# Planned attention steps with loads, first splits and conversions in the list, new due dates, and seven of ten banks of a pair split on GpSimd

## The chip, the cores and the metric

The kernel runs on one core of a Trainium2 chip. Its time is the device time of one execution in microseconds (us); less is better. Engines are called PE (matrix), DVE (vector), ACT (scalar), POOL (GpSimd) and SP (which issues the DMAs).

## What is computed

```python
scores = scale * np.matmul(q, k.transpose(0, 1, 3, 2))        # q, k, v: 4 x 8 heads x 576 x 64
thresh = np.max(scores, axis=-1, keepdims=True) - tau
scores = np.where(scores >= thresh, scores, -1000000000.0)
attn = softmax(scores)                                        # exp, sum, divide
x = (attn @ v), heads put side by side                        # 2304 tokens x 512
x = (silu(x @ w_gate) * (x @ w_val)) @ w_out                  # inner width 1536
out = (((x @ w1) * (x @ w2)) @ w3) @ w_out2                   # inner width 1024
```

The weights arrive as 64-bit floats, so each block of them is rebuilt as 32-bit values on the chip ("conversion"). Every matmul operand is split into a rounded part (hi) and the rest (lo), and products are summed from two or three matmuls.

## The kernel before

Attention takes two heads at a time, a *pair*: 16 pairs (4 batches of 4), 9 tiles of 128 query rows in each (four of head 0, one of both heads' last 64 rows, four of head 1), 144 tiles in all. A tile's chain is: `mm_scores` on PE into one of two double banks (L539), `el_max` on DVE (L571), the threshold (L580), `el_mask` on DVE (L587), which frees the bank, and `el_exp` on ACT (L596). A pair's probabilities are then transposed on PE (L425) into ten single banks, in the order four of head 0, `lq`, `kl`, four of head 1, and each bank is split into hi and lo in AT or ATL by one of three *paths*, named by one letter of `ROWS` (`plan_evac`):

- X: ACT copies hi (L891), DVE subtracts (L895);
- Y: ACT copies the bank to a tmp (L878), POOL rounds it (L184) and subtracts (L189);
- Z: ACT copies hi, PE subtracts it in the bank (`less`, L432), ACT copies lo (L902).

`plan_pv` then multiplies with v (L946, L958), ACT copies the result (L971), and SP stores it. For the next pair, `plan_turn` transposes q and k on PE, ACT makes hi (L813), DVE makes lo (L819), and `stack` issues four DMAs for k into R and eight for q into L (L448, L449), from which the next pair's scores read. `plan_left` does the last 64 rows of q and k, from `qkls`, which is split once in four pairs. `plan_split_v` splits v on POOL.

The order of all this, from the first pair's scores to the second tile of the last pair, comes from a list. `make_plan` gives each step an engine, a time for which it holds the engine (`busy`), a time after which its result may be used (`until`), the steps it waits for and a due date, counted in tiles (`z` is the pair's first tile). `Plan.order` goes through time and lets each engine take, among its next `AHEAD` steps by due date, the one that can start first, and of several the one that is due first:

```python
first = min(r[0] for r in ready)
t, due, k, step = min(
    (r for r in ready if r[0] <= first), key=lambda r: r[1:3]
)
```

The steps are then emitted in that order. On the chip each engine works through its own instructions in order and waits where an input isn't there. Ahead of the list stands a prologue (L756 to L772): the first loads, `first` (both heads of pair 0's k and q are split on DVE, transposed, copied to L and R), `split_left` and `it_left`. The last pair and everything behind it are emitted item by item. `plan_conv` is a weight block's conversion: an int part on DVE (L225, L228, L231), two activations on ACT, a subtract on POOL, a value on DVE (L257), a copy and a subtract (L299); three of the conversions (`EARLY`) stand in the list. Their loads are issued by `conv_fetch` within `begin` and `end`.

Of the kernel before, what the change touches and what calls it, by code (L numbers as in the profile page):

```python
# [33 lines left out]
ROWS, LAST = ("YZYYYXYYZX",), "XZ"  # L34


class Plan:
# [3 lines left out]
    HOP, AHEAD = 0.06, 60  # L41
# [16 lines left out]
    def order(self):  # L58
# [24 lines left out]
        while any(queues.values()):  # L83
            best = None
            for engine, q in queues.items():
                ready = []
                for due, k, step in q[:self.AHEAD]:
                    t = earliest(step, free[engine])
                    if t is not None:
                        ready.append((t, due, k, step))  # L90
                if not ready:
                    continue
                first = min(r[0] for r in ready)
                t, due, k, step = min(
                    (r for r in ready if r[0] <= first), key=lambda r: r[1:3]
                )
                if best is None or t < best[0]:
                    best = (t, engine, due, k, step)
# [15 lines left out]
def kernel(  # L114
# [177 lines left out]
    def conv_unit(src, key, **kw):  # L292
        def done(val):
# [5 lines left out]
            eng.tensor_tensor(out=un[:, 1, :], in0=val, in1=f32(un[:, 0, :]), op=ALU.subtract)  # L299
            wu[key] = un  # L300
        conv_push(src, done, **kw)
# [31 lines left out]
    def attention(actx, early, tail):  # L333
# [23 lines left out]
        def load_left(b):  # L357
            qk = ld.tile([P, H, D], F32, tag="qkl", name="qkl", bufs=1)
            vl = ld.tile([P, HP, D], F32, tag="vl", name="vl", bufs=1)
            nc.sync.dma_start(out=qk[0:64], in_=q[b, :, 512:S, :].rearrange("h p d -> p h d"))  # L360
            nc.sync.dma_start(out=qk[64:128], in_=k[b, :, 512:S, :].rearrange("h p d -> p h d"))
            vs = v[b, :, 512:S, :].rearrange("(g e) p d -> e p g d", e=2)
            for e in range(2):
                nc.sync.dma_start(out=vl[64 * e:64 * e + 64], in_=vs[e])
            lraw[b] = (qk, vl)
# [16 lines left out]

        def split_left(b):
            qk, vl = lraw.pop(b)
            qks = sp.tile([P, H, 3, D], F32R, tag="qkls", name="qkls", bufs=1)
            eng = nc.gpsimd if b else nc.vector
            for e in (0, 2):
                eng.tensor_scalar(
                    out=qks[:, :, e, :], in0=qk, scalar1=1.0, scalar2=1.0,
                    op0=ALU.mult, op1=ALU.mult,  # L390
                )
            eng.tensor_tensor(
                out=qks[:, :, 1, :], in0=qk, in1=f32(qks[:, :, 0, :]), op=ALU.subtract
            )
            for h in range(2):
                r = slice(64 * h, 64 * h + 64)
                split_pool(VLZ[b % 2][r, :, h, 0, :], VLZ[b % 2][r, :, h, 1, :], vl[r])
            lsplit[b] = qks
# [81 lines left out]


        def first(i, scale):
            L, R = qk_tiles(0)
            raw = raws.pop((0, i))
            for h in range(2):
                un = take()
                s5 = un.rearrange("p a b -> p (a b)")[:, 0:12 * D].rearrange(
                    "p (t s d) -> p t s d", t=4, s=3)
                src, hi = raw[:, h, :, :], s5[:, :, 0, :]
                for s in (0, 2):  # L490
                    nc.vector.tensor_scalar(
                        out=s5[:, :, s, :], in0=src, scalar1=scale, scalar2=None, op0=ALU.mult
                    )
                nc.vector.scalar_tensor_tensor(
                    out=s5[:, :, 1, :], in0=src, scalar=scale, in1=f32(hi),
                    op0=ALU.mult, op1=ALU.subtract,
                )
                s0 = (h + i + 1) % 2
                for n, a in enumerate((s0,) if i else (s0, 1 - s0)):
                    turn_r(  # L500
                        [s5[:, t, a:a + 2, :].rearrange("p s d -> p (s d)") for t in range(4)],
                        R[:, 640 * h:640 * h + 512] if i else L[:, 2 * n + h, :],
                    )
                give(un)

        def it_left(p):
            b, hp = divmod(p, HP)
            L, R = qk_tiles(p)
            qks = lsplit[b]
            bank = t_bank()  # L510
            br = bank.bitcast(F32R)
            for e in range(2):
                for h in range(2):
                    c = (2 * e + h) * P
                    s0 = (e + h + 1) % 2
                    src = qks[:, 2 * hp + h, s0:s0 + 2, :].rearrange("p a d -> p (a d)")
                    nc.tensor.transpose(br[:, c:c + P], src, ident_r)
            lz = LZ.rearrange("p e (h c) -> p e h c", c=192)[:, :, :, 0:64]
            bv = bank.rearrange("p (e h c) -> p e h c", e=2, h=2)
            scaled(lz, bv[:, :, :, 0:64], q_scale)  # L520
            scaled(R[:, 512:640].rearrange("p (h c) -> p h c", h=2), bv[:, 1, :, 64:P])
            scaled(R[:, 2 * S:2 * S + 64], bv[:, 1, 1, 64:P])
# [203 lines left out]
        def prep_items(p):  # L726
            b, hp = divmod(p, HP)
            return [lambda f=f: f(p) for f in (it_k, it_q, it_left)]

        def split_items(p):  # L730
            return [lambda: split_left(p // HP)] if p % HP == 0 else []

# [17 lines left out]
        def run_item(f):  # L750
# [4 lines left out]

        load(0, (1, 0))  # L756
        load_left(0)
        nc.scalar.dma_start(out=tau_sb, in_=tau.to_broadcast([P, 1]))

        nc.vector.tensor_scalar(  # L760
            out=q_scale, in0=tau_sb, scalar1=0.0, scalar2=0.125 / FAR, op0=ALU.is_ge, op1=ALU.mult
        )
        nc.vector.tensor_scalar(
            out=tau_sb, in0=tau_sb, scalar1=0.0, scalar2=None, op0=ALU.max
        )
# [102 lines left out]
        def plan_evac(path, b, a, due, hi, lo):  # L868
            if path == "Y":
                k = {}  # L870

                def raw():
# [18 lines left out]
                "ACT", 0.47, 0.6, [a], lambda: nc.scalar.copy(out=hi, in_=b["t"]), due + 0.1  # L891
            )
            if path == "X":
# [3 lines left out]
                    ), due + 0.3, closes=b,  # L897
                )
                return [c, d]
            d = plan.add("PE", 0.23, 0.45, [c], lambda: less(b["t"], hi), due + 0.2)  # L900
            e = plan.add(
                "ACT", 0.47, 0.6, [d], lambda: nc.scalar.copy(out=lo, in_=b["t"]), due + 0.3,  # L902
# [119 lines left out]
        def plan_split_left(b, due, war):  # L1022
            k = {}

            def qk_round(e):
                if not k:
                    k["qk"], k["vl"] = lraw.pop(b)
                    lsplit[b] = sp.tile([P, H, 3, D], F32R, tag="qkls", name="qkls", bufs=1)
                pool_round(lsplit[b][:, :, e, :], k["qk"])

            a = plan.add("POOL", 0.59, 0.63, war, lambda: qk_round(0), due)
            c = plan.add("POOL", 0.59, 0.63, [a], lambda: qk_round(2), due)
            d = plan.add("POOL", 1.25, 1.3, [c], lambda: pool_rest(
                lsplit[b][:, :, 1, :], k["qk"], lsplit[b][:, :, 0, :]), due)
            last = [d]
            for h in range(2):
                r = slice(64 * h, 64 * h + 64)
                hi, lo = (VLZ[b % 2][r, :, h, e, :] for e in range(2))
                last.append(plan.add(
                    "POOL", 0.38, 0.43, [last[-1]],  # L1040
                    lambda hi=hi, r=r: pool_round(hi, k["vl"][r]), due + 6 + h))
                last.append(plan.add(
                    "POOL", 0.72, 0.76, [last[-1]],
                    lambda hi=hi, lo=lo, r=r: pool_rest(lo, k["vl"][r], hi), due + 6 + h))
            return d, last[-1]

        def plan_split_v(p, due, war):
# [10 lines left out]
            if p + 2 < NP:  # L1058
                plan.add("SP", 0.1, 3.0, [c], lambda: load(p + 2, (2,)), due + 0.1)
            return c  # L1060

        def plan_conv(due):
# [7 lines left out]
            def end():  # L1070
# [552 lines left out]
```

## Time and profile before

| what | us |
|---|---|
| median of 3 runs | 1174.66 (1173.36 to 1178.68) |
| the profiled execution | 1175.01 |
| its span, first to last instruction | 1173.2 |
| PE busy / DVE busy / ACT busy / POOL busy | 1106.8 / 736.4 / 577.1 / 485.5 |

The span is 1.8 us shorter than the profiled execution's own time. "Busy" is the time in which an engine had an instruction under way; for PE the ends of matmuls are modelled, so a busy PE is not one at its peak. Attention is roughly the first 345 us; the rest are the two feed-forward stages.

### The profile page before, as it was taken

The page shows a single profiled execution, that of the slowest core. Times are in us where ns is not written, and L with a number is a line of the kernel's source. Part 1 is how long each engine was busy: PE and PEld are TensorE (multiplying, and loading weights), DVE is VectorE, ACT ScalarE, POOL GpSimd, SP SyncE. Part 2 cuts the span into 40 slices and gives each one's busy share as a digit, 9 for nine tenths or more (in the row PEclk, how much of TensorE's full clock was granted, in tenths as well). Part 3 has the DMA queues.
Part 4 walks back from the last instruction along what each step waited for, and adds up shares of the span by engine and source line. Part 5 has one row for each costly group of instructions (what it writes and reads, how often), then busy time and mean ns, then how long its engine had stood idle before and what let it go on. Part 6 is the DMA issues. An engine that isn't in the chain of part 4 may idle for free.

```text
span 1173.2 us, 16903 instructions
## 1 busy us (share of the span) xinstructions
PE 1106.8 (94%) x6008; PEld 957.4 (82%) x6008; DVE 736.4 (63%) x1300; ACT 577.1 (49%) x1151; POOL 485.5 (41%) x463
## 2 busy tenths in 40 slices
PE   5888899899988999999999999999899999999998
PEld 4778789898976877888888888888778888888886
DVE  6798999898885896756463655477991122522223
ACT  4687788888876356443341423245662231321111
POOL 2577587777643655443232333233332221321110
PEclk9898999999998999999999999999999999999999
DMA  4775766667655842222020211123330010100023
GB/s 99 176 179 129 174 153 165 161 144 171 144 176 137 237 117 90 72 72 72 19 72 19 68 58 36 42 84 113 111 112 7 1 37 1 37 1 1 1 61 101
DMA packets 105331, 107.09 MB, mean 91 GB/s; under 512 B 48288, under 2 KB 79648, under 8 KB 105248
## 3 DMA queue, kind: packets, MB, share of 16 engines
q1 hardware_dynamic: 105104, 106.01, 34.2%
q8 instruction: 48, 0.79, 0.3%
q14 instruction: 35, 0.29, 0.1%
q10 hardware_dynamic: 144, 0.00, 0.0%
HBM read 68.16 MB, written 14.23 MB: 70 GB/s over the span
## 4 chain that ended last, share of the span: by engine, by line
PE 55%; DVE 5%; DMA 1%; issue 1%; ACT 0%; POOL 0%; DVEq 0%; ACTq 0%
PE t_bank L1327 36%; PE s_bank L1327 19%; DMA raw<-in_moe_w_dram 1%; DVE tmp L257 1%; DVE slot L1310 1%; DVE raw L228 1%; DVE tmp L231 1%; DVE tmp L225 0%; DVE slot L1403 0%; DVE slot L299 0%; DVE slot L1512 0%; DVE slot L1374 0%; PE t_bank L1400 0%; DVE slot L1549 0%; POOL slot L299 0%
## 5 line engine op out<-in xcount | busy, mean ns | idle before, releaser
L1327 PE MATMUL t_bank<-slot,slot 128*128 128x512 f32 (+1 forms) x2592 | 561.3, 372 | 5.8 <-ACT slot L1309 2.0
L1327 PEld LDWEIGHTS t_bank<-slot,slot 128*128 128x128 f32 x2592 | 458.3, 189 | 93.0 <-ACT slot L1309 2.4
L1327 PE MATMUL s_bank<-h,slot 128*128 128x512 f32 (+1 forms) x720 | 163.3, 374 | 4.8 <-ACT h L192 2.9
L245 POOL TENSOR_TENSOR raw<-raw 128x512 int32<-128x512 int32 x76 | 83.6, 1101 | 167.5 <-ACT raw L240 158.2
L1327 PEld LDWEIGHTS s_bank<-h,slot 128*128 128x128 f32 x720 | 127.8, 191 | 29.2 <-ACT h L192 3.6
L1559 DVE TENSOR_TENSOR tmp<-tmp,t_bank 128x512 f32<-128x512 f32 (+1 forms) x40 | 25.3, 633 | 178.2 <-PE t_bank L1327 178.2
L193 POOL TENSOR_TENSOR h<-tmp,h 128x512 fp32r<-128x512 f32 (+1 forms) x60 | 74.4, 1241 | 141.2 <-ACT h L192 140.9
L1563 POOL TENSOR_TENSOR h<-tmp,h 128x512 fp32r<-128x512 f32 (+1 forms) x38 | 45.8, 1206 | 200.4 <-ACT h L1561 200.4
L571 DVE TENSOR_SCALAR_CACHE_REDUCE E<-s_bank 128x576 f32<-128x576 f32 x144 | 107.6, 753 | 32.3 <-PE s_bank L539 31.0
L596 ACT ACTIVATE P<-P,stat 128x576 f32<-128x576 f32 x144 | 113.8, 794 | 20.7 <-DVE P L587 20.0
L539 PE MATMUL s_bank<-R,L 128*128 128x288 f32 x512 | 101.1, 323 | 20.9 <-DVE P L587 11.4
L587 DVE SCALAR_TENSOR_TENSOR P<-E,stat,s_bank 128x576 f32<-128x576 f32 x144 | 114.5, 809 | 1.6
L189 POOL TENSOR_TENSOR AT<-tmp,AT 128x512 fp32r<-128x512 f32 x88 | 113.3, 1303 | 1.8
L1327 PE MATMUL s_bank<-slot,h 128*128 128x512 f32 x432 | 106.6, 391 | 0.9 <-DVE slot L1549 0.8
L1412 DVE TENSOR_TENSOR tmp<-tmp,t_bank 128x512 f32<-128x512 f32 (+1 forms) x60 | 37.9, 631 | 109.2 <-PE t_bank L1327 100.0
L539 PEld LDWEIGHTS s_bank<-R,L 128*128 128x128 f32 x512 | 78.6, 201 | 30.2 <-DVE P L587 9.5
L425 PE MATMUL t_bank<-ident,P 128*128 128x128 f32 x640 | 93.7, 281 | 4.6 <-ACT P L596 2.0
L1327 PEld LDWEIGHTS s_bank<-slot,h 128*128 128x128 f32 x432 | 80.0, 188 | 18.3 <-DVE slot L1549 2.1
L1374 DVE TENSOR_TENSOR slot<-s_bank,slot 128x1024 f32<-128x1024 f32 (+1 forms) x72 | 82.3, 1146 | 18.2 <-PE s_bank L1327 16.1
L184 POOL TENSOR_SCALAR AT<-tmp 128x512 fp32r<-128x512 f32 x88 | 55.2, 639 | 91.5 <-ACT tmp L878 84.3
L257 DVE SCALAR_TENSOR_TENSOR tmp<-tmp,raw 128x512 f32<-128x512 f32 x76 | 69.3, 912 | 34.1 <-POOL raw L245 34.1
L239 ACT ACTIVATE raw<-raw,ebias 128x512 int32<-128x512 int32 x76 | 58.1, 764 | 63.0 <-DVE tmp L231 43.4
(131 smaller groups left out, 1398.8 us busy)
## 6 DMA issues: line engine op xcount, KB each, us to landing
raw<-in_moe_w_dram SPq DMA_DIRECT2D x32, 512.0 KB, 3.6
raw<-in_moe_w_out_dram SPq DMA_DIRECT2D x20, 512.0 KB, 3.5
x_dram<-xs SPq DMA_DIRECT2D x64, 144.0 KB, 2.7
L<-qlo SPq DMA_DIRECT2D x60, 128.0 KB, 2.4
L<-qhi SPq DMA_DIRECT2D x60, 128.0 KB, 2.4
raw<-in_moe_w_gate_dram SPq DMA_DIRECT2D x12, 512.0 KB, 4.1
raw<-in_moe_w_val_dram SPq DMA_DIRECT2D x12, 512.0 KB, 3.5
ld<-in_k_dram SPq DMA_DIRECT2D x16, 256.0 KB, 3.9
```

The lines of the kernel that those rows point to most:

```text
L189: nc.gpsimd.tensor_tensor(out=lo, in0=src, in1=f32(hi), op=ALU.subtract)
L193: nc.gpsimd.tensor_tensor(out=lo, in0=src, in1=f32(hi), op=ALU.subtract)
L239: nc.scalar.activation(out=a, in_=x, func=ACTF.Relu, scale=8.0, bias=ebias[:, 0:1])
L245: nc.gpsimd.tensor_tensor(out=a, in0=a, in1=x, op=ALU.subtract)
L257: nc.vector.scalar_tensor_tensor(out=f32(m), in0=f32(m), scalar=2.0 ** 20, in1=f32(a), op0=ALU.add, op1=ALU.mult)
L425: nc.tensor.matmul(bank[:, t * P:(t + 1) * P], lhsT=part, rhs=ident, is_transpose=True, start=(t == 0), stop=(t == len(parts) - 1),)
L539: nc.tensor.matmul(o, lhsT=lhs, rhs=R[:, c:c + HALF], start=(h == hs2[0] and e == 0), stop=(h == hs2[-1] and e == 1),)
L571: nc.vector.tensor_scalar(out=halves(t), in0=sb[:, :, 0:HALF], scalar1=-FAR, scalar2=None, op0=ALU.mult, op1=ALU.min, accum_out=st[:, 0, c],)
L587: nc.vector.scalar_tensor_tensor(out=halves(p_tile(p, i)), in0=halves(t), scalar=st[:, 1, c], in1=sb[:, :, 0:HALF], op0=ALU.is_gt, op1=ALU ...
L596: nc.scalar.activation(out=u, in_=u, func=ACTF.Exp, scale=-FAR, bias=st[:, 0, c], accum_out=sums[p // HP][:, c],)
L1327: nc.tensor.matmul(o, lhsT=lhs(a), rhs=rhs(c), start=(first and i == 0), stop=(last and i == 2))
L1374: nc.vector.tensor_tensor(out=a, in0=s, in1=a, op=ALU.add)
```

## The change

`ROWS` goes from YZYYYXYYZX to YZYYYZYYYX: of a pair's ten banks, `kl` goes from X to Z, the third bank of head 1 from Z to Y; seven instead of six take path Y, one instead of two path X, two path Z as before. Nearly all due dates are new numbers (the table `W`), and a step is chosen among 400 instead of 60. The prologue is gone: the first loads (k of pair 0, its left rows, q, then v and pair 1's k, q and v), the split of pair 0's k and q head by head, and the left rows' split are steps of the list; two heads of the left rows are split on DVE, the other six and v's left rows on POOL. The first four tiles wait for head 0's operands alone. The next pair's turn of k and q is due about 1.6 and 2.5 tiles earlier. A conversion's load is an SP step of its own, due four tiles ahead, and the last subtract of a conversion is a step of its own on POOL or DVE. The lists' waits for v's loads, and the holding times of the conversion's DVE steps (2.2 for 1.7, 1.0 for 0.6), are new. `load_left` can load q and k's part or v's part alone.

```diff
--- before.py
+++ after.py
-ROWS, LAST = ("YZYYYXYYZX",), "XZ"
+ROWS, LAST = ("YZYYYZYYYX",), "XZ"
+W = {
+    "s": 4.05, "two": 0.98, "exp": 1.03, "k": -0.14, "q": 0.47, "left": 5.44, "sqk": 8.68,
+    "svl": 12.52, "sv": 5.9, "T0": 5, "t0": 0.47, "lq": 7.39, "co": 6.31, "kl": 8.43, "T1": 9.6,
+    "t1": 1.02, "pv": 12.69, "ph": 1.95, "pn": 0.8, "norm": 15.36, "conv": 5.29, "raw": -0.18,
+    "pool": -0.49, "x": -0.09, "z": -1.39,
+}
-    HOP, AHEAD = 0.06, 60
+    HOP, AHEAD = 0.06, 400
...
-                    (r for r in ready if r[0] <= first), key=lambda r: r[1:3]
+                    (r for r in ready if r[0] <= first + 1e-9), key=lambda r: r[1:3]
...
-        load(0, (1, 0))
-        load_left(0)
...
-        first(1, 1.0)
-        first(0, q_scale)
-        split_left(0)
-        it_left(0)
-        load(0, (2,))
-        load(1, (1, 0))
-        load(1, (2,))
...
+        def plan_split_qk(b, due, war, heads, engine, cost):
...
+            a = plan.add(engine, cost, cost + 0.05, war, lambda: both(0), due)
+            c = plan.add(engine, cost, cost + 0.05, [a], lambda: both(2), due)
+            return plan.add(engine, 2 * cost, 2 * cost + 0.1, [c], rest, due)
...
+        def plan_first(i, h, due, deps):
...
+            a = plan.add("DVE", cost, cost + 0.08, deps, lambda: rounds(0), due)
+            c = plan.add("DVE", cost, cost + 0.08, [a], lambda: rounds(2), due)
+            d = plan.add("DVE", 0.34, 0.42, [a], rest, due)
...
+                x = plan_bank(b, due + 0.01 * n, 0.5, [c, d], fill)
...
+                ends.append(plan.add("ACT", 0.47, 0.6, [x], out, due + 0.02, closes=b))
+            return ends, x
+
+        def plan_start():
+            sp_at = lambda cost, land, emit: plan.add("SP", cost, land, [], emit, -20)
+            k0 = sp_at(1.5, 5.1, lambda: load(0, (1,)))
+            l0 = sp_at(0.15, 4.8, lambda: load_left(0, (0,)))
+            q0 = sp_at(0.1, 5.6, lambda: load(0, (0,)))
+            v0 = sp_at(0.15, 6.0, lambda: load_left(0, (1,)))
+            w0 = sp_at(0.1, 6.9, lambda: load(0, (2,)))
+            k1 = sp_at(0.1, 7.8, lambda: load(1, (1,)))
+            q1 = sp_at(0.1, 8.7, lambda: load(1, (0,)))
+            w1 = sp_at(0.1, 9.6, lambda: load(1, (2,)))
...
+            kh0, x = plan_first(1, 0, -8, [k0])
+            left = plan_split_qk(0, -7.5, [l0], slice(0, 2), "DVE", 0.13)
+            qh0, _ = plan_first(0, 0, -7, [q0, qs])
+            left0 = plan_left(0, -6.5, [left])
+            kh1, _ = plan_first(1, 1, -3, [k0])
+            qh1, _ = plan_first(0, 1, -2, [q0, qs, x])
+            rest = plan_split_qk(0, -1, [l0, left], slice(2, H), "POOL", 0.46)
+            vl = plan_split_vl(0, 2, [v0])
+            return kh0 + qh0 + [left0], kh1 + qh1, rest, vl
...
-        def plan_conv(due):
+        def plan_conv(due, engine, deps):
...
-            a = plan.add("DVE", 1.7, 1.8, [], begin, due, opens=r)
+            ld = plan.add("SP", 0.1, 4.5, deps, conv_fetch, due - 4)
+            a = plan.add("DVE", 2.2, 2.3, [ld], begin, due, opens=r)
...
-            e = plan.add("DVE", 0.6, 0.68, [d], end, due + 1)
-            f = plan.add("ACT", 0.47, 0.6, [e], lambda: k["rest"][0](k["val"]), due + 1.2)
-            plan.add("POOL", 1.25, 1.3, [f], None, due + 1.4, closes=r)
+            e = plan.add("DVE", 1.0, 1.1, [d], value, due + 1)
+            f = plan.add("ACT", 0.47, 0.6, [e], copy, due + 1.2)
+            plan.add(engine, 1.25, 1.3, [f], lambda: k["lo"](), due + 1.4, closes=r)
...
-                    score[n] = plan.add("PE", big, big + 0.17, deps, go, n - 3)
+                    score[n] = plan.add("PE", big, big + 0.17, deps, go, n - W["s"])
...
-                rk = plan_turn(q, 1, z + (1.5 if p else 3), soon + ready[p][:1])
-                rq = plan_turn(q, 0, z + (3 if p else 4), soon + ready[p][1:2])
+                rk = plan_turn(q, 1, z + W["k"], soon)
+                rq = plan_turn(q, 0, z + W["q"], soon)
...
-                    lefts[b] = plan_split_left(b, z + 7, [left_done[q], ld])
-                vdone = plan_split_v(p, z + 6, [pv.get(("pv", p - 2)), score[z]])
+                    lefts[b] = plan_split_qk(b, z + W["sqk"], [left_done[q], ld], slice(0, H), "POOL", 0.6)
+                    vls[b] = plan_split_vl(b, z + W["svl"], [ld])
+                vdone = plan_split_v(
+                    p, z + W["sv"], [pv.get(("pv", p - 2)), score[z], landed.get((p, 2))])
...
-                    plan_conv(z + 6)
+                    plan_conv(
+                        z + W["conv"], "DVE" if EARLY.index(p) % 2 else "POOL", [score[z]])
```

## Rows read from the trace of the kernel before

**Rows 1.** The page, part 1: busy us, share of the span, instructions.

```profile
PE 1106.8 (94%) x6008; PEld 957.4 (82%) x6008; DVE 736.4 (63%) x1300; ACT 577.1 (49%) x1151; POOL 485.5 (41%) x463
```

**Rows 2.** Windows: start and end, length, busy by engine, granted clock, DMA share, GB/s.

```profile
0.00:15.52 15.52, 6.35 (x33) 5.18 (x34) 9.03 (x25) 5.32 (x10) 5.53 (x12) 1.00 0.83 167
15.52:36.77 21.25, 13.89 (x77) 12.18 (x77) 14.77 (x36) 11.12 (x28) 7.70 (x9) 0.97 0.37 83
36.77:321.72 284.95, 258.07 (x1898) 244.63 (x1897) 256.59 (x595) 234.30 (x567) 199.22 (x218) 0.96 0.68 158
321.72:345.60 23.88, 21.59 (x146) 19.42 (x145) 21.01 (x47) 18.92 (x45) 12.19 (x11) 1.00 0.59 188
345.60:1173.20 827.60, 806.90 (x3861) 675.98 (x3859) 435.00 (x599) 307.45 (x504) 260.82 (x215) 0.99 0.21 64
```

**Rows 3.** Windows of three single pairs: the fourth, the fifth and the seventh.

```profile
82.41:99.49 17.08, 16.83 (x132) 16.20 (x131) 16.40 (x40) 15.48 (x39) 16.37 (x19) 1.00 0.68 150
99.49:124.76 25.27, 21.86 (x148) 20.62 (x146) 22.07 (x47) 18.16 (x46) 14.63 (x17) 0.86 0.56 127
...
146.83:164.34 17.51, 17.12 (x132) 16.16 (x131) 16.20 (x40) 15.22 (x38) 14.01 (x17) 1.00 0.76 175
```

**Rows 4.** Waits of DVE, 36.77 to 321.72: total us, times, longest.

```profile
DVE E L571 <- PE s_bank L539: 23.9, 31, 3.7
DVE tmp L225 <- DMA raw<-in_moe_w_gate_dram: 2.1, 1, 2.1
```

**Rows 5.** Waits of PE, 36.77 to 321.72: total us, times, longest.

```profile
PE s_bank L539 <- DVE P L587: 18.0, 15, 4.2
PE s_bank L539 <- DMA L<-qlo: 3.0, 3, 1.7
```

**Rows 6.** Timeline where pair 10 begins: start, us, instruction, idle before it.

```profile
225.59 0.66 PE L539 MATMUL s_bank<-R,L 128*128 128x288 f32 x3 [1.67 <-DMA L<-qlo]
...
226.29 0.76 DVE L571 TENSOR_SCALAR_CACHE_REDUCE E<-s_bank 128x576 f32<-128x576 f32 x1 [3.71 <-PE s_bank L539]
```

**Rows 7.** Timeline of pair 0 and the begin of pair 1.

```profile
1.25 0.46 SPq L378 DMA_DIRECT2D ld<-in_q_dram  x1
...
5.23 0.29 DVE L491 TENSOR_SCALAR slot<-ld 128x256 fp32r<-128x256 f32 x1 [1.15 <-DMA ld<-in_k_dram]
...
10.80 0.61 PE L539 MATMUL s_bank<-R,L 128*128 128x288 f32 x1 [0.17 <-ACT L L479]
...
15.52 0.76 DVE L571 TENSOR_SCALAR_CACHE_REDUCE E<-s_bank 128x576 f32<-128x576 f32 x1 [3.50 <-PE s_bank L539]
...
26.75 0.54 SPq L448 DMA_DIRECT2D R<-khi  x1
...
34.44 0.60 SPq L449 DMA_DIRECT2D L<-qhi  x1
...
35.68 1.06 PE L539 MATMUL s_bank<-R,L 128*128 128x288 f32 x3 [2.10 <-DMA L<-qlo]
...
36.77 0.76 DVE L571 TENSOR_SCALAR_CACHE_REDUCE E<-s_bank 128x576 f32<-128x576 f32 x1 [3.32 <-PE s_bank L539]
```

**Rows 8.** Timeline around the first conversion in the list.

```profile
57.71 0.81 DVE L225 TENSOR_SCALAR tmp<-raw 128x512 int32<-128x512 int32 x1 [2.12 <-DMA raw<-in_moe_w_gate_dram]
...
62.37 0.91 PE L539 MATMUL s_bank<-R,L 128*128 128x288 f32 x4 [4.15 <-DVE P L587]
```

**Rows 9.** Single lines, 15 to 322: count, shortest/median/longest ns, first and last start.

```profile
L587 DVE SCALAR_TENSOR_TENSOR P<-E,stat,s_bank x135: 799/809/818, 17.4 to 321.0; 128x576 f32<-128x576 f32 x135
L895 DVE TENSOR_TENSOR AT<-t_bank,AT x14: 678/684/692, 48.0 to 311.3; 128x512 fp32r<-128x512 f32 x14
L184 POOL TENSOR_SCALAR AT<-tmp x85: 611/623/1058, 27.9 to 318.4; 128x512 fp32r<-128x512 f32 x85
L189 POOL TENSOR_TENSOR AT<-tmp,AT x85: 1265/1290/1730, 28.6 to 319.1; 128x512 fp32r<-128x512 f32 x85
L231 DVE SCALAR_TENSOR_TENSOR tmp<-raw,tmp x3: 675/1746/1751, 59.8 to 185.7; 128x512 f32<-128x512 uint16 x3
```

More of the change, by code (lines that the diff above doesn't have):

```diff
@@ L298, in done @@
             eng = nc.gpsimd if conv_i[0] % 2 else nc.vector
-            eng.tensor_tensor(out=un[:, 1, :], in0=val, in1=f32(un[:, 0, :]), op=ALU.subtract)
             wu[key] = un
+            rest = lambda: eng.tensor_tensor(
+                out=un[:, 1, :], in0=val, in1=f32(un[:, 0, :]), op=ALU.subtract
+            )
+            return rest if later else rest()
         conv_push(src, done, **kw)
@@ L355, in attention, with load_left @@
         stats, sums, pbuf = {}, {}, {}
[L357 to L365, printed above, removed]
+        def load_left(b, which=(0, 1)):
+            if 0 in which:
+                t = ld.tile([P, H, D], F32, tag="qkl", name="qkl", bufs=1)
+                nc.sync.dma_start(out=t[0:64], in_=q[b, :, 512:S, :].rearrange("h p d -> p h d"))
+                nc.sync.dma_start(out=t[64:128], in_=k[b, :, 512:S, :].rearrange("h p d -> p h d"))
+                lraw[b, 0] = t
+            if 1 in which:
+                t = ld.tile([P, HP, D], F32, tag="vl", name="vl", bufs=1)
+                vs = v[b, :, 512:S, :].rearrange("(g e) p d -> e p g d", e=2)
+                for e in range(2):
+                    nc.sync.dma_start(out=t[64 * e:64 * e + 64], in_=vs[e])
+                lraw[b, 1] = t
         def load(p, which):
@@ L381, in load @@
                 raws[p, i] = t
[L383 to L398, printed above, removed]
         def split_v(p):
@@ L479, in turn_r @@
             nc.scalar.copy(out=dst, in_=bank)
[L482 to L522, printed above, removed]
         def mm_scores(p, i):
@@ L890, in plan_evac @@
             c = plan.add(
-                "ACT", 0.47, 0.6, [a], lambda: nc.scalar.copy(out=hi, in_=b["t"]), due + 0.1
+                "ACT", 0.47, 0.6, [a], lambda: nc.scalar.copy(out=hi, in_=b["t"]), due + W["raw"]
             )
@@ L896, in plan_evac @@
                         out=lo, in0=b["t"], in1=f32(hi), op=ALU.subtract
[L897 removed]
+                    ), due + W["x"], closes=b,
                 )
                 return [c, d]
[L900 removed]
+            d = plan.add("PE", 0.23, 0.45, [c], lambda: less(b["t"], hi), due + W["z"])
             e = plan.add(
[L902 removed]
+                "ACT", 0.47, 0.6, [d], lambda: nc.scalar.copy(out=lo, in_=b["t"]), due + W["x"],
                 closes=b,
@@ L1020, in plan_norm, with both, rest, plan_split_vl @@
             plan.add("SP", 0.2, 3.0, [d], store, due + 0.2)
[L1022 to L1027, printed above, removed]
-                    lsplit[b] = sp.tile([P, H, 3, D], F32R, tag="qkls", name="qkls", bufs=1)
[L1029 to L1035, printed above, removed]
+        def plan_split_qk(b, due, war, heads, engine, cost):
+            def both(e):
+                if b not in lsplit:
+                    lsplit[b] = sp.tile([P, H, 3, D], F32R, tag="qkls", name="qkls", bufs=1)
+                out, in_ = lsplit[b][:, heads, e, :], lraw[b, 0][:, heads, :]
+                if engine == "POOL":
+                    pool_round(out, in_)
+                else:
+                    nc.vector.tensor_scalar(
+                        out=out, in0=in_, scalar1=1.0, scalar2=None, op0=ALU.mult
+                    )
+            def rest():
+                eng = nc.gpsimd if engine == "POOL" else nc.vector
+                eng.tensor_tensor(
+                    out=lsplit[b][:, heads, 1, :], in0=lraw[b, 0][:, heads, :],
+                    in1=f32(lsplit[b][:, heads, 0, :]), op=ALU.subtract,
+                )
+            a = plan.add(engine, cost, cost + 0.05, war, lambda: both(0), due)
+            c = plan.add(engine, cost, cost + 0.05, [a], lambda: both(2), due)
+            return plan.add(engine, 2 * cost, 2 * cost + 0.1, [c], rest, due)
+        def plan_split_vl(b, due, war):
+            last = war
             for h in range(2):
@@ L1038, in plan_split_left @@
                 hi, lo = (VLZ[b % 2][r, :, h, e, :] for e in range(2))
[L1039 to L1045, printed above, removed]
+                last = [plan.add(
+                    "POOL", 0.38, 0.43, last,
+                    lambda hi=hi, r=r: pool_round(hi, lraw[b, 1][r]), due + h)]
@@ new lines, in plan_split_vl, with rounds, rest, fill @@
+                last = [plan.add(
+                    "POOL", 0.72, 0.76, last,
+                    lambda hi=hi, lo=lo, r=r: pool_rest(lo, lraw[b, 1][r], hi), due + h)]
+            return last[0]
+        def plan_first(i, h, due, deps):
+            k = {}
+            scale = 1.0 if i else q_scale
+            cost = 0.2 if i else 0.26
+            def rounds(s):
+                if not k:
+                    k["un"] = take()
+                    k["s5"] = k["un"].rearrange("p a b -> p (a b)")[:, 0:12 * D].rearrange(
+                        "p (t s d) -> p t s d", t=4, s=3)
+                nc.vector.tensor_scalar(
+                    out=k["s5"][:, :, s, :], in0=raws[0, i][:, h, :, :], scalar1=scale,
+                    scalar2=None, op0=ALU.mult,
+                )
+            def rest():
+                nc.vector.scalar_tensor_tensor(
+                    out=k["s5"][:, :, 1, :], in0=raws[0, i][:, h, :, :], scalar=scale,
+                    in1=f32(k["s5"][:, :, 0, :]), op0=ALU.mult, op1=ALU.subtract,
+                )
+            a = plan.add("DVE", cost, cost + 0.08, deps, lambda: rounds(0), due)
+            c = plan.add("DVE", cost, cost + 0.08, [a], lambda: rounds(2), due)
+            d = plan.add("DVE", 0.34, 0.42, [a], rest, due)
+            s0 = (h + i + 1) % 2
+            ends = []
+            halves_of = (s0,) if i else (s0, 1 - s0)
+            for n, at in enumerate(halves_of):
+                b = plan.res("bank")
+                def fill(bank, n=n, at=at):
+                    for t in range(4):
+                        nc.tensor.transpose(
+                            bank.bitcast(F32R)[:, t * P:(t + 1) * P],
+                            k["s5"][:, t, at:at + 2, :].rearrange("p s d -> p (s d)"), ident_r,
+                        )
+                    if n == len(halves_of) - 1:
+                        give(k["un"])
+                x = plan_bank(b, due + 0.01 * n, 0.5, [c, d], fill)
+                def out(n=n, b=b):
+                    L, R = qk_tiles(0)
+                    dst = R[:, 640 * h:640 * h + 512] if i else L[:, 2 * n + h, :]
+                    nc.scalar.copy(out=dst, in_=b["t"])
+                ends.append(plan.add("ACT", 0.47, 0.6, [x], out, due + 0.02, closes=b))
+            return ends, x
```

84 lines of the change are left out of this document (36 added, 48 removed).

## Prediction

> **What bounds the kernel now.** The page's busy shares come first [rows 1], but they mix two programs: behind 345.6 us PE is busy 806.9 of 827.6 us [rows 2], and nothing of that part is edited. What the change can move lies ahead of it. So the second view is the windows, cut where a pair's first row maximum starts on DVE. Pair 0 takes 36.8 us with everything ahead of it, pairs 1 to 14 take 284.95 us (20.35 each), the last one up to the feed-forward's first stretch 23.9 us [rows 2]. In the fourteen pairs DVE is busy 256.6 of 285 us (90%), PE 258.1 (91%, at a granted clock of 0.96), ACT 234.3 (82%), POOL 199.2 (70%) [rows 2]. No engine is full. The reader is to see two things there: DVE and PE are nearly level, and POOL has 85.7 us left, 6.1 a pair.
>
> The third view is single pairs. The fourth takes 17.08 us and the seventh 17.51, the fifth 25.27, all with the same banks and paths [rows 3]. In the quick ones PE is busy all but 0.25 and 0.4 us, DVE all but 0.7 and 1.3 us [rows 3]. So about 17 us is what the engines' work of a pair takes when the orders fit, and the 3 us between that and 20.35 are waits.
>
> The fourth view says which. DVE waits 23.9 us in 31 places for scores, and 2.1 us for one weight block [rows 4]. PE in turn waits 18.0 us in 15 places for the mask that frees a bank, and 3.0 us for the stacked q [rows 5]: scores late, then masks late, in turns. When PE idles, its clock falls: in the fifth pair it was 0.86 on average, in the quick ones 1.00 [rows 3]. A mean of 0.96 over 285 us, between the levels 1.2 and 2.4 GHz, is 23 us at the lower one (0.04 x 285 / 0.5), in which about 11 us of PE's work is lost. Fewer idles give some of it back.
>
> **The change part by part, worked on the profiled execution, 1175.0 us** (1173.2 of span and 1.8 around it; the median of the runs is 0.35 lower, which is nothing here).
>
> *Paths.* One X less a pair takes one 0.684 us subtract from DVE [rows 9]. The two Z stay two, so PE's and ACT's work is the same: X and Y have one ACT copy each, Z two, twelve before and after. One Y more puts 0.623 + 1.290 = 1.91 us on POOL [rows 9]. On DVE, fourteen pairs make -9.6 us, and with DVE at 90% in a ring with PE I take all of it. POOL goes from 14.2 (199.2 / 14) to 16.1 us a pair; its cover is the 6.1 us of idle, of which 2.5 are left if a pair takes 18.6. The cost is 0 there. If the last split of head 1 ended last ahead of the product with v, it would be 1.91 each pair, 26.7 us in all.
>
> *The banks' split moving to POOL, against a rule.* First the row: with POOL busy 70% of the time, 135 masks took 799 to 818 ns [rows 9], so not one was held up by POOL; the conversion's L231 took 675 at best and 1746 in the middle, and POOL's own two operations reach 1058 and 1730 [rows 9]. So the engines do get in each other's way, but in the conversions' steps. The Trainium skill, page "Perfetto Trace Analysis", section "Optimizing Scalar/DVE Operations", warns that DVE and GpSimd share a port into SBUF, so that moving work from the one to the other may not help. This case's trace agrees for L231 alone, and speaks against it for the masks (799 to 818 ns). The sum goes by the row, 0; by the rule's word 26.7 us would go back on DVE, a rival below.
>
> *Earlier turn of k and q.* Twelve DMAs per pair stay twelve, 7.7 us of SP from the first issue to the last [rows 7], landing after that. Before, they end so late that pair 1's scores wait 2.1 us and DVE 3.3 [rows 7]; in pair 10 PE waits 1.67 and DVE 3.71 [rows 6]. Due two tiles earlier, 4 us at 2.0 to 2.3 us a tile, they should land before the pair begins. What is queued behind them on SP are stores of the results and loads two pairs ahead, which have a pair's time. I take off pair 1's 3.3 (in the start's sum) and 5 us in the fourteen pairs: pair 10's 3.7 and something for the other two waits of PE on q. Bounds: 3 (PE's own waits [rows 5]) and 8.
>
> *Conversions.* Load as a step of its own: the 2.1 us wait of DVE goes [rows 4, 8]; behind it stood a mask, and PE waited 4.15 us for that [rows 8]. The conversion's work stays: three blocks, the same two on POOL and one on DVE. The longer holding times only let the list leave room. I take -2.1, bounds 0 and -4.
>
> *Other due dates, 400 steps in view.* This has no row of its own. Of DVE's 28.4 us of idle (284.95 - 256.59), 2.1 and 5 are gone above; about 21 are left, mostly 0.2 to 2 us each behind scores. Below stands no gain at all; above, all pairs at the mean of the quick ones, 17.3. Scores due four tiles ahead, not three, stand earlier in PE's order, which is what DVE waits for in 31 places; but the wider view also lets work be pulled up whose input on the chip is late. I take -3, near the lower end.
>
> *Start.* Before, the first score starts at 10.8 us and the first maximum at 15.5 [rows 7], because both heads of k and q and the whole of qkls are split first. After, only head 0's k and q, and two heads of the left rows. The counter-cost: q's load is fourth instead of second on SP, some 1.3 us later than 1.25 us [rows 7] (estimate: two more issues of some 0.65, by the spacing in [rows 7]). k lands at 5.2 [rows 7], q at some 7; then 1 us of splits, 1.3 of transposes, 1.1 of copies, 0.6 of the first score and its latency: the first maximum at 12, 3.5 earlier (estimate). Head 1's splits, 2.3 us of DVE, go behind it; DVE idles 21.25 - 14.77 = 6.5 us up to 36.77 [rows 2], which covers half. POOL splits the other six heads at that time; the two can hold each other up as in L231, by about 1 us each time (1746 - 675). Sum: -3.5 - 3.3 + 1.8 = -5.0; bounds +1 and -8.
>
> *Sum.* -9.6 - 5 - 2.1 - 3 - 5.0 = -24.7; the last pair and the rest start earlier and stay as long. 1175.0 - 24.7 = **1150 us**. A pair would take 18.9 us (20.35 - 19.7 / 14), still over the 17 of the quick ones. Its own range is the unknown terms at both ends: 1164 with the weakest (start 0, turn 3, nothing for due dates, 1 for the load, two thirds of DVE's part: 10.4), 1138 with the strongest (start 8, turn 8, load 4, due dates 8, DVE 9.6: 37.6).
>
> **The rivals.**
> A whole fit: every pair runs as the quick ones. 14 x (20.35 - 17.3) = 42.7, and 5 at the start: 1127. For it: two of fourteen do it today [rows 3]. Against it: neighbours with the same list's rules take 25.
> POOL ends last: YYYX at the end of head 1 puts three splits in a row of 1.91 ahead of the product with v, where YYZX had two; 26.7 us go back, 1175 - 24.7 + 26.7 = 1177, no change that can be told. Against it: 6.1 us of idle a pair.
> The shared port: each added split holds DVE as long as it lasts, the same 26.7 and 1177. Against it: the masks' 818 ns at most.
> Work pulled up too early, the other side: with 400 steps in view an engine takes a step whose input on the chip comes later than the list assumed, as the first conversion did, where DVE stood 2.1 us and PE 4.15 [rows 8]. Each such place costs 4.15. Six of them eat the gain; from nine on it is slower beyond measure, 1175 - 24.7 + 9 x 4.15 = 1188. For it: DMAs, 0.6 us an issue, twelve in a row in 7.7 us [rows 7], where the list holds SP 0.5 for each of the two stacks. Against it: the earlier turn gives just these some 4 us more.
>
> **How the numbers follow.** Forecast 0.60, whole fit 0.14, POOL last 0.11, shared port 0.04, too early 0.11. What can be told from no change on this kernel is about 0.5%, 6 us. Faster 0.60 + 0.14 = 0.74, the same 0.15, slower 0.11. The range reaches from 1128, with most of the whole fit, to 1177, where POOL last and port stand, and leaves out the slower case and a little below.
>
> **What would show it.** Right: the first maximum near 12 us; the fourteen pairs near 265 us, with DVE busy some 247 and POOL some 226; no wait of L539 for stacked q; PE's clock in that stretch nearer 1.00; masks still about 809 ns; the last part still about 828 us long. Wrong: POOL over 95% in the pairs with PE waiting for its lo parts before L946; DVE idle ahead of L225 or a turn; SP's stacks in front of a load that a transpose waits for; masks of 1.5 us and more.

## The result and the profile after

The changed kernel took 1143.14 us (median of four, 1139.82 to 1148.41) beside 1174.99 for the kernel before: ratio 0.9729, 95% interval 0.9678 to 0.9779. The forecast was 1150, so the direction and about four fifths of the gain were foreseen (24.7 of 31.9 us). The profiled execution took 1140.14 us, 34.9 less than the one shown before. One execution of 3257.28 us, of the kernel with 60 steps in view, lies outside all others and is left out below.

Windows of the changed kernel, cut as in [rows 2] where a pair's first maximum starts (start and end, length, busy by engine with the count of instructions, granted clock, DMA share, GB/s):

```profile
0.00:14.04 14.04, 5.61 (x33) 5.09 (x34) 9.16 (x24) 5.32 (x10) 6.64 (x15) 1.00 0.87 177
14.04:31.24 17.20, 12.63 (x77) 11.60 (x77) 14.85 (x36) 11.49 (x28) 6.40 (x8) 0.90 0.62 139
31.24:286.69 255.45, 244.61 (x1889) 233.90 (x1888) 247.97 (x582) 231.03 (x568) 228.23 (x247) 1.00 0.74 176
```

Pairs 1 to 14 take 255.45 us, 18.25 each, where they took 284.95 [rows 2]: 29.5 us. Pair 1 begins at 31.24, not 36.77: 5.5 us. From there to the end it is as long as before: 1138.3 - 286.69 = 851.6 us beside 1173.2 - 321.72 = 851.5. Within the fourteen pairs DVE's busy time fell by 8.6 us, and its idle time from 28.4 to 7.5: most of the gain is idle time. PE's busy time fell by 13.5 us with hardly fewer instructions (1889 for 1898), at a granted clock of 1.00 (0.96 before): the prediction expected the clock to give some time back, but had no term for it. DVE is now busy 97% of these pairs, PE 96%, POOL 89%.

Waits in those pairs, DVE, PE, then POOL (total us, times, longest), to set beside [rows 4, 5]:

```profile
DVE E L524 <- PE s_bank L492: 3.4, 13, 0.6
...
PE s_bank L492 <- DVE P L540: 7.7, 10, 1.4
...
PE t_bank L874 <- POOL AT L196: 0.5, 1, 0.5
...
POOL AT L191 <- ACT tmp L806: 20.7, 24, 3.4
```

DVE's wait for scores went from 23.9 to 3.4 us, PE's for the mask from 18.0 to 7.7. No wait for stacked q is left in this execution, and POOL, busy 2.1 us a pair more, held PE up once, for 0.5 us. The single lines that answer to [rows 9] (count, shortest/median/longest ns):

```profile
L540 DVE SCALAR_TENSOR_TENSOR P<-E,stat,s_bank x135: 717/810/818, 15.7 to 285.9; 128x576 f32<-128x576 f32 x135
...
L196 POOL TENSOR_TENSOR AT<-tmp,AT x99: 1270/1292/1742, 25.9 to 284.6; 128x512 fp32r<-128x512 f32 x99
...
L238 DVE SCALAR_TENSOR_TENSOR tmp<-raw,tmp x3: 1089/1092/1776, 75.4 to 187.2; 128x512 f32<-128x512 uint16 x3
```

The masks (L540) are as fast as before, 810 ns in the middle for 809, with POOL busy 89% of the time instead of 70%. The start, in order of time (start, us, instruction, idle before it):

```profile
4.96 0.29 DVE L996 TENSOR_SCALAR slot<-ld 128x256 fp32r<-128x256 f32 x1 [0.88 <-DMA ld<-in_k_dram]
...
9.11 1.30 DVE L996 TENSOR_SCALAR slot<-ld,q_scale 128x256 fp32r<-128x256 f32 x1
...
10.22 1.03 POOL L964 TENSOR_TENSOR qkls<-qkl,qkls 128x384 fp32r<-128x384 f32 x1
10.33 1.21 DVE L1002 SCALAR_TENSOR_TENSOR slot<-ld,q_scale,slot 128x256 fp32r<-128x256 f32 x1
...
11.69 1.23 PE L1018 MATMUL t_bank<-ident_r,slot 128*128 128x128 f32 x8 [1.18 <-DVE slot L1002]
...
12.71 2.25 PE L492 MATMUL s_bank<-R,L 128*128 128x288 f32 x8
...
14.04 0.76 DVE L524 TENSOR_SCALAR_CACHE_REDUCE E<-s_bank 128x576 f32<-128x576 f32 x1 [2.50 <-PE s_bank L492]
```

The first maximum is at 14.04 us, not near 12: head 1's q was still transposed ahead of the first score (the eight transposes at 11.69), and DVE's splits took longer while POOL split the left rows (L996 1.30 us instead of 0.29 for one shape, L1002 1.21 beside L964, 0.42 at its shortest). Most of what is saved comes after: pair 0 takes 17.2 us, not 21.25, with 2.4 us of DVE idle for 6.5.

### The profile page after: what moved, and what is told of

Same layout as the page of the kernel before. It is cut to its first block, busy times and chain, and to the rows that moved or that the text cites. A ratio compares the mean times of both kernels' runs of the same rounds, so it can differ in the third digit from the quotient of the medians.

```text
span 1138.3 us, 16926 instructions
## 1 busy us (share of the span) xinstructions
PE 1091.1 (96%) x6008; PEld 945.4 (83%) x6008; DVE 729.7 (64%) x1286; ACT 574.0 (50%) x1151; POOL 514.2 (45%) x494
## 4 chain that ended last, share of the span: by engine, by line
PE 57%; DVE 5%; DMA 2%; issue 1%; ACT 0%; POOL 0%; DVEq 0%; ACTq 0%
PE t_bank L1340 37%; PE s_bank L1340 19%; DMA raw<-in_moe_w_dram 2%; DVE tmp L264 1%; DVE slot L1323 1%; DVE raw L235 1%; DVE tmp L238 1%; DVE tmp L232 0%; DVE slot L307 0%; DVE slot L1416 0%; PE t_bank L1413 0%; DVE slot L1525 0%; DVE slot L1387 0%; DVE slot L1562 0%; POOL slot L307 0%
## 5 line engine op out<-in xcount | busy, mean ns | idle before, releaser
L252 POOL TENSOR_TENSOR raw<-raw 128x512 int32<-128x512 int32 x76 | 83.8, 1104 | 166.0 <-ACT raw L247 162.7
L196 POOL TENSOR_TENSOR AT<-tmp,AT 128x512 fp32r<-128x512 f32 x102 | 132.5, 1309 | 3.6
L540 DVE SCALAR_TENSOR_TENSOR P<-E,stat,s_bank 128x576 f32<-128x576 f32 x144 | 114.6, 809 | 1.6
L492 PE MATMUL s_bank<-R,L 128*128 128x288 f32 x512 | 95.4, 310 | 11.8 <-DVE P L540 9.4
L1340 PEld LDWEIGHTS s_bank<-slot,h 128*128 128x128 f32 x432 | 80.0, 188 | 18.3 <-DVE slot L1562 2.1
L421 PE MATMUL t_bank<-ident,P 128*128 128x128 f32 x640 | 91.3, 277 | 2.1 <-ACT P L549 1.6
L492 PEld LDWEIGHTS s_bank<-R,L 128*128 128x128 f32 x512 | 74.4, 191 | 19.0 <-DVE P L540 7.2
L264 DVE SCALAR_TENSOR_TENSOR tmp<-tmp,raw 128x512 f32<-128x512 f32 x76 | 69.5, 916 | 32.0 <-POOL raw L252 31.9
L1424 ACT ACTIVATE tmp<-t_bank 128x512 f32<-128x512 f32 (+1 forms) x60 | 33.2, 553 | 108.1 <-PE t_bank L1340 101.7
```

The costliest lines, as they stand in the source:

```text
L196: nc.gpsimd.tensor_tensor(out=lo, in0=src, in1=f32(hi), op=ALU.subtract)
L252: nc.gpsimd.tensor_tensor(out=a, in0=a, in1=x, op=ALU.subtract)
L264: nc.vector.scalar_tensor_tensor(out=f32(m), in0=f32(m), scalar=2.0 ** 20, in1=f32(a), op0=ALU.add, op1=ALU.mult)
L421: nc.tensor.matmul(bank[:, t * P:(t + 1) * P], lhsT=part, rhs=ident, is_transpose=True, start=(t == 0), stop=(t == len(parts) - 1),)
L492: nc.tensor.matmul(o, lhsT=lhs, rhs=R[:, c:c + HALF], start=(h == hs2[0] and e == 0), stop=(h == hs2[-1] and e == 1),)
L540: nc.vector.scalar_tensor_tensor(out=halves(p_tile(p, i)), in0=halves(t), scalar=st[:, 1, c], in1=sb[:, :, 0:HALF], op0=ALU.is_gt, op1=ALU ...
```

## The experiments

All medians are of three or more executions; ratios are to the kernel before on the same chip, with 95% intervals. Differences in us to the changed kernel's 1143.1 set runs beside each other that were not all on the same chip. The changed kernel run again, beside the last three kernels below, gave 1142.6 us (ratio 0.9719, 0.968 to 0.9757).

**The paths alone, undone and done.**

```diff
-ROWS, LAST = ("YZYYYZYYYX",), "XZ"
+ROWS, LAST = ("YZYYYXYYZX",), "XZ"
```

> The changed kernel with the paths YZYYYXYYZX of before. If the one subtract less a pair is paid in full, DVE is 9.6 us longer in fourteen pairs: about 1153 us. If DVE isn't what sets the pace (rival), no difference that can be told: 1143 us. If the dates fit only the new paths (rival): over 1158 us.

Measured: 1150.4 us (0.9784, 0.9753 to 0.9815), 7.3 us above the changed kernel's 1143.1. The same edit the other way in the kernel before:

> The kernel before with the new paths YZYYYZYYYX and nothing else. If DVE's work sets the pace, 9.6 us less than before: about 1165 us. Rival: with the old dates DVE's idle time grows by what its work falls, since PE and DVE wait for each other in turns: no change that can be told, 1170 to 1180 us.

Measured: 1168.9 us (0.994, 0.992 to 0.9959), 7.3 us below its own 1176.2. Its fourteen pairs and DVE's waits for scores there, then the fourteen pairs of the changed kernel with the old paths:

```profile
36.90:316.15 279.25, 256.55 (x1898) 242.70 (x1897) 246.65 (x581) 232.98 (x568) 223.97 (x245) 0.97 0.69 160
DVE E L571 <- PE s_bank L539: 24.7, 26, 5.0
...
31.39:294.27 262.88, 248.68 (x1884) 233.64 (x1883) 251.99 (x595) 233.00 (x567) 201.66 (x218) 1.00 0.73 172
```

In the kernel before, DVE's work fell by 9.9 us (256.59 to 246.65) and its waits for scores stayed (23.9 to 24.7). Not all of it came through: the pairs are 5.7 us shorter (284.95 to 279.25), for DVE's idle time as a whole rose from 28.4 to 32.6, a part of what the rival said. In the changed kernel the old paths make DVE busy only 4.0 us longer and idle 3.4 us longer. Both ways the paths are worth about 7 us, with either set of dates, less than the 9.6 of the sum. The first difference by itself is hardly clear of the noise (the two intervals overlap); the second is.

**All due dates as before.** The table `W` holds the old numbers:

```diff
-    "s": 4.05, "two": 0.98, "exp": 1.03, "k": -0.14, "q": 0.47, "left": 5.44, "sqk": 8.68,
-    "svl": 12.52, "sv": 5.9, "T0": 5, "t0": 0.47, "lq": 7.39, "co": 6.31, "kl": 8.43, "T1": 9.6,
-    "t1": 1.02, "pv": 12.69, "ph": 1.95, "pn": 0.8, "norm": 15.36, "conv": 5.29, "raw": -0.18,
-    "pool": -0.49, "x": -0.09, "z": -1.39,
+    "s": 3, "two": 1, "exp": 0.5, "k": 1.5, "q": 3, "left": 5.5, "sqk": 7,
+    "svl": 13, "sv": 6, "T0": 5, "t0": 0.6, "lq": 7.6, "co": 8, "kl": 9.2, "T1": 9.6,
+    "t1": 0.5, "pv": 12, "ph": 1.6, "pn": 0.8, "norm": 15.2, "conv": 6, "raw": 0.1,
+    "pool": 0.2, "x": 0.3, "z": 0.2,
```

> The changed kernel with the due dates of before in the table W, all else as changed. By the prediction's sum the due dates are worth the turn's 5 us and 3 us more: about 1151 us, the fourteen pairs near 264 us. Rival: the dates are most of the gain, because DVE's waits for scores fell from 23.9 to 3.4 us in those pairs: about 1163 us or more, the pairs over 275 us, with DVE waits for scores of 15 us and more.

Measured: 1160.6 us (0.9876, 0.9832 to 0.992), 17.5 above. Its windows and DVE's waits in the fourteen pairs:

```profile
31.90:303.25 271.35, 250.83 (x1898) 238.02 (x1897) 249.75 (x583) 232.74 (x572) 229.29 (x250) 0.99 0.70 164
...
DVE E L524 <- PE s_bank L492: 13.3, 28, 1.5
DVE tmp L232 <- DMA raw<-in_moe_w_gate_dram: 2.2, 1, 2.2
```

The outcome lies nearer the rival (1163 us or more, pairs over 275, waits of 15 and more) than the sum (1151, 264), though short of it. DVE's work is the same as after within 2 us, and the waits for scores (13.3 for 3.4 us) and for a weight block (2.2) are back. So the dates as a set are the larger part of the gain. Of the 15.9 us that the fourteen pairs are longer, 4.5 and 3.7 are in the two pairs with the first and the second conversion (25.14 for 20.66 us, 24.04 for 20.34), at a granted clock of 0.93 in both; no conversion step took over 1.76 us there. The start stays quick (pair 1 begins at 31.90), so that comes from the planned start and not from the dates.

**Parts of the dates.** First the scores' date, then the turn's, then the split steps':

```diff
-    "s": 4.05,
+    "s": 3,
```

> The changed kernel with the scores due three tiles ahead, as before, not 4.05. If DVE waited for scores because they stood late in PE's order, most of the 17 us come back: 1152 us or more, DVE's waits for scores over 10 us in the fourteen pairs. If the other dates make room for them: 1143 to 1148 us.

```diff
-    "k": -0.14, "q": 0.47,
+    "k": 1.5, "q": 3,
```

> The changed kernel with the next pair's turn of k and q due at 1.5 and 3 tiles, as before, not -0.14 and 0.47. By the prediction's sum 5 us more, 1148 us, with scores waiting for the stacked q again. Rival: no difference, 1143 us, as the run with all dates of before had no long wait for it either.

```diff
-    "raw": -0.18, "pool": -0.49, "x": -0.09, "z": -1.39,
+    "raw": 0.1, "pool": 0.2, "x": 0.3, "z": 0.2,
```

> The changed kernel with the four dates of a bank's split steps as before (ACT's copy +0.1, POOL's steps +0.2, the second subtract +0.3, PE's subtract +0.2 tiles behind the bank's date, instead of -0.18, -0.49, -0.09, -1.39). If these dates are most of what the whole table was worth (17 us), 1155 us or more; if they are one of many small ones, 1143 to 1148 us.

Measured: scores 1150.1 us (0.9779, 0.973 to 0.9827), turn 1146.6 (0.9746, 0.9704 to 0.9787), split steps 1152.1 (0.9796, 0.9756 to 0.9837). For the turn no wait on stacked q came back, and its 3.5 us can't be told from nothing. For the other two neither expectation fits, for most of the loss sits in one place. Pair 6, which has the second conversion (pairs are counted from 0, as in the code), from its first maximum to the next pair's: after, then with the scores' date, then with the split steps':

```profile
121.72:142.06 20.34, 18.67 (x144) 17.51 (x143) 20.20 (x45) 18.93 (x45) 19.44 (x22) 1.00 0.82 200
...
122.45:150.98 28.53, 20.82 (x149) 19.36 (x148) 27.87 (x45) 19.90 (x48) 22.11 (x24) 0.89 0.54 126
...
123.03:150.33 27.30, 21.71 (x150) 20.68 (x149) 25.16 (x45) 19.27 (x46) 20.74 (x24) 0.87 0.60 140
```

Of the 9.9 and 8.9 us that their fourteen pairs are longer, 8.2 and 7.0 are in this pair. DVE there, with the split steps' dates:

```profile
129.00 0.73 DVE L235 TENSOR_SCALAR raw<-raw 128x512 int32<-128x512 int32 x1
129.65 6.32 DVE L238 SCALAR_TENSOR_TENSOR tmp<-raw,tmp 128x512 f32<-128x512 uint16 x1
135.89 0.74 DVE L747 SCALAR_TENSOR_TENSOR qlo<-t_bank,q_scale,qhi 128x512 fp32r<-128x512 f32 x1
```

and POOL in the same microseconds of the same kernel:

```profile
129.42 0.57 POOL L191 TENSOR_SCALAR VLZ<-vl 64x256 fp32r<-64x256 f32 x1
129.96 1.27 POOL L196 TENSOR_TENSOR AT<-tmp,AT 128x512 fp32r<-128x512 f32 x1
131.21 1.19 POOL L191 TENSOR_SCALAR AT<-tmp 128x512 fp32r<-128x512 f32 x2
132.37 2.47 POOL L196 TENSOR_TENSOR AT<-tmp,AT 128x512 fp32r<-128x512 f32 x2
134.82 0.61 POOL L191 TENSOR_SCALAR AT<-tmp 128x512 fp32r<-128x512 f32 x1
137.65 1.04 POOL L252 TENSOR_TENSOR raw<-raw 128x512 int32<-128x512 int32 x1 [2.23 <-ACT raw L247]
```

L238 takes 0.68 us when left alone (675 ns at best [rows 9]). POOL's unbroken row of work ends at 135.43 us, and L238 ends 0.54 us later. POOL stopped there because its next step (L252) waits, by way of ACT (L247), for L238 itself. With the scores' date it is L264, which ends 0.55 us after a row of POOL's:

```profile
137.76 8.45 DVE L264 SCALAR_TENSOR_TENSOR tmp<-tmp,raw 128x512 f32<-128x512 f32 x1
146.13 0.74 DVE L524 TENSOR_SCALAR_CACHE_REDUCE E<-s_bank 128x576 f32<-128x576 f32 x1
```

Each hold-up was seen in one profiled execution; the other executions of either kernel took as long within 0.7 us, but what they hold was not seen.

**The last subtract off DVE.**

```diff
-ROWS, LAST = ("YZYYYZYYYX",), "XZ"
+ROWS, LAST = ("YZYYYZYYYZ",), "XZ"
```

> The changed kernel with path Z in place of the one X left (YZYYYZYYYZ). DVE is busy 97% of the fourteen pairs; if it alone sets the pace, 9.6 us less: about 1134 us. If ACT (231 us busy, 8.4 us more by this) or PE (3.2 us more) are the next limit, between 1138 and 1146 us.

Measured: 1149.95 us (0.9781, 0.9739 to 0.9822), neither of the two expectations: slower than the changed kernel by about 7 us, though DVE is busy only 241.33 us in the fourteen pairs. DVE's waits for scores rose to 17.8 us, and one step was held up in pair 6 (25.88 us) once more:

```profile
32.27:295.54 263.27, 245.96 (x1888) 235.97 (x1887) 241.33 (x567) 236.13 (x578) 225.09 (x245) 0.99 0.72 168
DVE E L524 <- PE s_bank L492: 17.8, 41, 1.7
...
130.38 5.95 DVE L235 TENSOR_SCALAR raw<-raw 128x512 int32<-128x512 int32 x1
```

L235 takes 0.43 us where it is left alone. Of the 7.8 us that the fourteen pairs are longer, 5.5 are in pair 6, so most of the loss is this hold-up and not the path. But the other thirteen pairs took 237.4 us, no less than the changed kernel's 235.1, with the waits for scores spread over all of them. So less work on DVE didn't pay by itself.

**The view.**

```diff
-    HOP, AHEAD = 0.06, 400
+    HOP, AHEAD = 0.06, 60
```

> The changed kernel with 60 instead of 400 steps in view. By the prediction a small term, within 3 us of 1143 us. Rival: the wide view is what fills DVE's and PE's idle time: over 1155 us.

Measured: ratio 0.9747 (0.9705 to 0.9788); the profiled execution took 1141.95 us, two others 1147.47 and 1148.40. The fourteen pairs take 255.50 us, as after. In both traces every engine has the same instructions in the same order: with 60 steps in view the list comes out as with 400. The wide view is worth nothing here.

These are thus three more executions of the changed kernel. With its ten others they lie between 1139.08 and 1149.10 us, none of them between 1143.06 and 1146.15. The six long ones have a mean granted clock of 0.987 to 0.991, the seven short ones 0.991 to 0.996; which is the cause of the other isn't shown.

**Where the conversions stand.** Pair 6 is also one in which POOL splits a batch's left rows. Two kernels have the conversions elsewhere, with the new dates and with the split steps' old ones, and the changed kernel ran beside them:

```diff
-EARLY = (3, 6, 9)
+EARLY = (1, 5, 9)
```

> The changed kernel with the three conversions of the list in pairs 1, 5 and 9 instead of 3, 6 and 9, so that none falls in a pair in which POOL also splits a batch's left rows (2, 6, 10). If the long hold-ups come from POOL's unbroken work in pair 6, no conversion step over 2 us, times in one place, about 1140 us. Rival: a conversion is held up wherever it stands, and the times are those of the changed kernel.

> The kernel with the old dates of a bank's split steps (1152 us, with one conversion step of 6.3 us in pair 6) and the conversions in pairs 1, 5 and 9. If the hold-up is what those dates cost, some 7 us come back: 1145 us or less. If the dates themselves cost it: 1152 us.

> The changed kernel once more, beside the runs that follow. Its four times so far lie in two places, 1140 (twice) and 1146 to 1148. If those are the second conversion's DVE step held up by POOL in some executions and not in others, the times fall in two places again; a profile of a long one shows a conversion step of 5 us and more in pair 6. Rival: plain scatter, with times all over 1139 to 1149.

Measured: the changed kernel with conversions moved 1145.64 us (0.9731, 0.9703 to 0.976), six times from 1144.62 to 1146.09: in one place, as expected, but not at 1140. The old split dates with conversions moved 1146.57 (0.9738, 0.9703 to 0.9774), near the 1145 of a loss by the hold-up. In neither does a conversion step of the list take over 1.76 us. So the old split dates cost 0.9 us where no step is held up, which can't be told from nothing, and 5.6 of the 9 us they seemed to cost went with the hold-up. Moving the conversions didn't pay for the changed kernel itself, whose profiled executions have no hold-up (longest step 1.78 us). Run again, it took 1142.6 us, six times from 1139.08 to 1149.1; the profiled one, of 1142.13, showed no hold-up either. Whether its longer executions hold one is open: all that were profiled are short ones.

Without conversions in the list:

```diff
-EARLY = (3, 6, 9)
+EARLY = ()
```

> The changed kernel without conversions in the list; the three blocks are converted behind it. In the fourteen pairs DVE has some 11 us less to do, and no step of it has two inputs that POOL could hold up: 244 us or less for the fourteen pairs (255.5 now), times in one place. The whole may be longer than 1143 us, as the feed-forward's begin waits for the three blocks.

Measured: 1138.03 us (0.9669, 0.9634 to 0.9704), four times from 1137.04 to 1139.12. This is the fastest kernel of the study, by 4.6 us against the changed one on the same chip. Its fourteen pairs, DVE's waits for scores in them, and a stretch of the last pair:

```profile
31.20:278.36 247.16, 241.71 (x1889) 233.29 (x1888) 235.98 (x570) 226.07 (x559) 219.49 (x242) 1.00 0.74 172
DVE E L524 <- PE s_bank L492: 7.5, 18, 0.7
...
300.00:310.00 10.00, 6.27 (x20) 4.86 (x21) 10.00 (x22) 8.05 (x18) 5.64 (x5) 0.54 0.41 120
...
303.50 2.26 PE L492 MATMUL s_bank<-R,L 128*128 128x288 f32 x8 [5.00 <-DVE P L540]
```

8.3 us less than after, 17.65 a pair. 5.3 us of it go back behind them (1135.3 - 278.36 = 856.9 us for 851.6). The expectation put that on the feed-forward's begin; the trace shows it earlier, in the last pair, where the blocks are converted now: DVE is busy without a break from 300 to 310 us, and PE waits 5.0 us for a mask there, at a granted clock of 0.54. The expected 244 us were too few: DVE's waits for scores rose to 7.5 us.

## Why the prediction was right, step by step

The way and the range were right, and what the gain mostly consists of stood in the sum: fewer DVE subtracts, a quicker start, and less idle time of DVE behind scores. The sizes of the first and the last were off in opposite ways. What the runs give for the paths (7.3), the dates (17.5) and the start (5.5) adds up to 30.3 of the 31.9 us, though parts that are undone one by one need not add up.

- **Paths, -9.6 us.** Right in kind, too large. DVE's busy time fell by 8.6 us, and undoing or doing the paths alone changed the time by about 7.
- **POOL's cover, 0.** Right: 16.3 us a pair (forecast 16.1), with one wait of 0.5 us on it. POOL last is out as a rival.
- **Shared port, 0.** Right for the masks, 717 to 818 ns with POOL busy 89%. The warning of the Trainium skill, page "Perfetto Trace Analysis", section "Optimizing Scalar/DVE Operations", is still borne out in another place: DVE's conversion steps and the start's splits. In the changed kernel they lost up to 1.1 us each, about as the prediction had bounded it; in three kernels close to it one step took 5.95 to 8.45 us.
- **Turn, -5 us.** The sign was right, the size isn't confirmed. The waits for stacked q are gone (0 for 3.0 us), but they were also gone with the turn's old dates, alone and with all the others; undoing the turn's cost 3.5 us, within the noise. With the new paths alone in the kernel before, these waits were 1.0 us. What removed the rest was not tried.
- **Load step, -2.1 us.** No DVE wait for a weight block after. With all old dates it came back (2.2 us) although the load was still a step of its own, so the step alone doesn't do it. It came back with none of the three groups of dates that were tried singly; which date removes it is open.
- **Due dates, -3 us.** This is the term that was mis-sized. All dates together, the turn's and the load's with them, are worth 17.5 us where the sum had 3 + 5 + 2.1 = 10.1. The forecast of DVE's work was close (247 us, 247.97 measured), that of its idle time was not: 265 - 247 leaves 18 us, and 7.5 were measured. 9.9 of the 15.9 us that the old dates add to the fourteen pairs are waits for scores. Most of two single dates' losses was one held-up step each, so the worth of each date alone is not settled.
- **Start, -5.0 us.** Right in sum, 5.5 measured, but by luck, not in its parts: 1.5 for 3.5 us at the first maximum, and the rest from pair 0 running with fewer waits. In two other executions of the same instructions pair 1 began at 32.6 and 33.0 us, which makes it 3.7 to 5.5.
- **The slower rival**, a step pulled up ahead of its input by the wide view: it did not happen, and couldn't, as 60 and 400 steps give the same order.
- **The whole fit**, 17.3 us a pair, was not reached: 18.25, or 17.65 without conversions. It rested on a reading that was wrong. The two quick pairs differ from the fifth not only in waits: the fifth has a conversion's first steps in it (L225 at 121.02 us), the quick ones have none, and DVE is busy 22.07 us in it beside 16.40 and 16.20 [rows 3]. Over the fourteen pairs DVE's work alone was 18.3 us a pair before and by the prediction's own 247 us 17.6 after, so 17.3 was out of reach.

## What to carry to other kernels

Where several engines are each busy about 90% and wait for each other in turns, the order in which one engine serves the others can be worth more than the work that is moved: here 17.5 us by dates and about 7 by work. Test a single date with care, since a loss may be one unlucky meeting of two instructions: look for a step that takes ten times its usual time before ascribing the loss to the date. Where DVE steps that only touch SBUF stand in a stretch in which POOL is busy without a break, try them elsewhere: here that gave 5.6 us back where a step had been held up, nothing where none was, and 4.6 us with all of them behind the stretch.

## What the runs showed of the hardware that was not expected

A DVE step with its operands in SBUF can wait for more than one POOL instruction. In three kernels it ended only after an unbroken row of them: L238 took 6.32 us (0.68 alone), L264 8.45 (0.68), L235 5.95 (0.43), and each ended 0.3 to 0.6 us after POOL had run out of work. In the other cases such a step took at most 2.1 us, the length of one POOL instruction or two. What decides between the two was not found. The Trainium skill, page "SBUF — State Buffer", section "Who interferes with whom", has the one of the two that comes second blocked while the other holds the pair of ports they share for its whole instruction. Read as a wait for one instruction, that would be at most 1.3 us here, and the runs show seven in a row for L238 and ten for L264. That the shared ports are the cause is argued from this and not tested by itself.
